# A written-out schedule drawn again: new prices for transfers in the planner, one warm-up matmul fewer, fifteen search seeds in place of four

## The chip, the cores and the metric

One core of one Trainium2 chip runs the whole program in one launch. The metric is the device time of a run in microseconds (us), smaller is better. The kernel before takes 506.23 us as the median of three runs (504.22 to 507.21). TensorE is called PE, VectorE DVE, ScalarE ACT, GpSimd POOL, SyncE SP.

## The reference

Causal attention over 2 batches of 12 heads (448 positions, head size 64), followed by two feed-forward layers over the 896 tokens of 768 features, with 2048 hidden units each:

```python
scores = scale * q @ k.T;  scores = where(mask, -1e9, scores)
attn = exp(scores - max) / (sum + 1e-09);  x = attn @ v          # 896 x 768
h = x @ w_in;  x = (h * clip(h + 3, 0, 6) / 6) @ w_out           # layer 1
h = x @ w_in2; y = (max(h, 0) + alpha * min(h, 0)) @ w_out2      # layer 2
```

## The kernel before

**Precision and tiling.** Scores, transposes and attention products run on PE as f32 matmuls, which the trace shows as two records each. The two layers run on f32r halves: a value is split into a high and a low part, and a product is three matmuls (`three`: high·high, low·high, high·low), each 128 weights columns by 448 tokens. Both layers use a scheme with 7 products of half-size blocks in place of 8, so that blocks of x, of the weights and of the hidden values (`g`) are first added to or subtracted from each other.

**Names.** Attention: `s`, `sl` scores, `e`, `el` their exponentials, `t`, `r` transposes, `a` the transposed exponentials, `o` the output of a head pair. Products into a layer (`w_in`, 8 steps `m`): operands `b11`, `t1`, `t2`, ... against weights `a1`, `s12`, ... in the PSUM banks `a`, `b`, `c`. Products out of a layer (`w_out`) are numbered 1, 2, 7, 6, 4, 5, 3 and run in that order, 72 matmuls each, over operands `x1..`, `x2..`, `x7..` and so on (`x70` to `x77` for product 7; the suffix h or l is the high or the low part) and weights `w1`, `w2`, `w7`, ... into three banks `ya` (products 1, 6, 5, 3), `yb` (2) or `yc` (7, 4). There are 8 banks in all, so the third `yc` bank is the first `yb` bank that comes free: after product 2 DVE adds `yb` to `y` (L770), and frees it.

**Sums.** Before product 7, 6 and 4 the `g` blocks are added to each other in place (`add_g`, 8 sums of 128x448 each), and so are weight blocks. `add_on` (L299 to L312) lets either DVE do such a sum (L309), or POOL issue a transfer that adds on landing (L307). A weight arrives as 64-bit words: SP loads it (`raw`, 768 KB), ACT makes two passes (L262, L265), DVE one (L268), before it is split into halves (ACT L283, DVE L290).

**What sets the order.** Nothing is ordered by hand. Each step is an `Op` with engines it may run on, a price on each of them in us, its operands and a due time. `Plan.solve` walks through a simulated time with these prices: at each step it takes, over all engines, the earliest step that is ready and has its buffers, by due time where several are. `on` with several engines is settled there too. The due times and engine choices of the attention steps (`vary`) are disturbed by random draws, one for each number in `SEEDS`, on top of each other. The resulting list is then emitted, and each engine runs its part of it strictly in order, waiting on semaphores. So a price changes no instruction's work, only where it stands and, for some, on which engine. The prices of transfers are `ISSUE`, `WAIT` and `SHARE` (L64 to L76), read by `lands_at`. Three warm-up matmuls on zeros (`WARM`, L803) stand first on PE.

Of the kernel before, what the change touches and what calls it, by code (L numbers as in the profile page):

```python
# [32 lines left out]
PE, DVE, ACT, POOL, SP = "PE", "DVE", "ACT", "POOL", "SP"  # L33


def f32(t):
    return t.bitcast(F32)
# [12 lines left out]
class Op:  # L50
# [7 lines left out]
    def lands(self, *load, on=SP):  # L58
# [2 lines left out]

ISSUE, WAIT = 0.9, {384: 6.0, 448: 6.5, 768: 7.0}  # L64

TURN = {("r", "r"): 0.05, ("r", "t"): 0.17, ("r", "c"): 0.2, ("r", "q"): 0.15, ("r", "m"): 0.15, ("t", "r"): 0.12,
        ("t", "c"): 0.12, ("t", "q"): 0.1, ("m", "c"): 0.2, ("m", "r"): 0.1, ("m", "q"): 0.1}
LAG = {PE: 0.20, DVE: 0.12, ACT: 0.15, POOL: 0.10, SP: 0.04}
FAR = 1.0e6

SHARE = 3.5

EARLY = 3.0


def lands_at(on, first, us, landed):  # L76

    return max(first, landed[on], min(landed[POOL if on == SP else SP], first + SHARE)) + us

class Plan:
# [30 lines left out]
    def solve(self, slots, strict, overlay, vary=0, seeds=()):  # L113

        for i, o in enumerate(self.ops):
            o.index = i
            for p in o.before:
                p.after.append(o)
        for o in reversed(self.ops):
# [22 lines left out]
        first = {}  # L142
# [4 lines left out]
        queue = {c: sorted((b for b in first if b.cls == c), key=first.get) for c in strict}  # L147
        waiting = {o: len(o.before) for o in self.ops}
        ready = {e: [] for e in LAG}
        clock, landed, port = dict.fromkeys(LAG, 0.7), {SP: 0.0, POOL: 0.0}, 0.0  # L150

        def put(o):
            o.ready = {}
            for e, _ in o.on:
                o.ready[e] = max([p.out + (LAG[p.eng] if p.eng != e else 0.0) for p in o.before], default=0.0)
                ready[e].append(o)

        for o in self.ops:
# [3 lines left out]
        while len(done) < len(self.ops):  # L162
            best = None
            room = {c: queue[c][:len(free[c])] for c in strict}
            for e in LAG:
                can = []
                for o in ready[e]:
                    t = max(clock[e] + TURN.get((mode, o.mode), 0.0) if e == PE else clock[e], o.ready[e])
                    if (e == POOL and e not in o.dma) or (e == DVE and o.port):
                        t = max(t, port)  # L170
                    ok = True
                    need = {}
                    for b in o.bufs:
                        if b.slot is None:
                            need[b.cls] = need.get(b.cls, 0) + 1
                            f = free[b.cls]
                            if len(f) < need[b.cls] or (b.cls in room and b not in room[b.cls]):
                                ok = False
                                break
                            t = max(t, sorted(f)[need[b.cls] - 1][0])  # L180
                    if ok and len(o.on) > 1:
                        def done_by(x, us):
                            late = max(clock[x], o.ready[x], port if (x == POOL and x not in o.dma) or (x == DVE and o.port) else 0.0)
                            late += bias[x] if x != o.on[0][0] else 0.0
                            return lands_at(x, late + o.load[0], o.load[1], landed) if x in o.dma else late + us

                        if POOL in o.dma and done_by(*o.on[0]) + o.on[-1][1] <= o.due - EARLY:
                            ok = e == POOL
                        else:
                            ok = e == min(o.on, key=lambda c: done_by(*c))[0]  # L190
                    if ok:
                        can.append((t, o))
                if can:
                    soon = min(can, key=lambda r: r[0])[0] + hold
                    t, o = min((r for r in can if r[0] <= soon), key=lambda r: (r[1].due, r[1].index))
                    key = (round(t, 2), o.due)
                    if best is None or key < best[0]:
                        best = (key, e, o, t)
            if best is None:
                raise RuntimeError("no step is possible: %s" % [  # L200
                    (e, o.on, [b.name for b in o.bufs]) for e in LAG for o in sorted(ready[e], key=lambda o: o.due)[:4]
                ])
            _, e, o, t = best
            for x, _ in o.on:
                ready[x].remove(o)
            o.eng, o.start = e, t
            mode = o.mode if e == PE else mode
            o.out = o.end = clock[e] = t + dict(o.on)[e]
            if (e == POOL and e not in o.dma) or (e == DVE and o.port):
                port = o.end  # L210
            if o.load and e in o.dma:
                wait, us = o.load
                o.out = landed[e] = lands_at(e, o.start + wait, us, landed)
            for b in [b for b in o.bufs if b.slot is None]:
                f = free[b.cls]
                k = min(range(len(f)), key=lambda i: f[i][0])
                b.slot = f.pop(k)[1]
                if b.cls in strict:
                    queue[b.cls].remove(b)
            for b in o.bufs:  # L220
                b.left -= 1
                b.end = max(b.end, o.out + LAG[e])
                if not b.left:
                    free[b.cls].append((b.end, b.slot))
            if any(b.cls in over_of for b in o.bufs):
                over_left -= 1
                over_end = max(over_end, o.end)
                if not over_left:
                    n = slots[over_cls]
                    free[over_cls] += [(over_end, n + i) for i in range(over_n)]  # L230
            for s in o.after:
                waiting[s] -= 1
                if not waiting[s]:
                    put(s)
            done.append(o)
# [3 lines left out]
class Kernel:  # L239
# [9 lines left out]
    def convert(self, src, sign=1.0, halves=False):  # L249

        nc, op = self.nc, self.plan.op
        raw = Buf("raw", "raw", 2 * DM, U32)
        w = Buf("w", "wf", DM, U32)
        keys = [(w, 0), (w, W3)] if halves else [w]

        def words(k):
            return raw.tile.rearrange("p (n two) -> p n two", two=2)[:, :, k]

        op((SP, 0.45), lambda e: nc.sync.dma_start(out=raw.tile, in_=src), writes=[(raw, "l"), (raw, "h")]).lands(3.2, 2.4)


        op((ACT, 0.80), lambda e: nc.scalar.activation(  # L262
            f32(w.tile), f32(words(1)), AF.Prelu, scale=sign * 2.0 ** -112, alpha=-2.0 ** 32), reads=[(raw, "h")], writes=keys)

        op((ACT, 0.81), lambda e: nc.scalar.activation(  # L265
            words(0), raw.tile.bitcast(U16).rearrange("p (n four) -> p n four", four=4)[:, :, 1],
            AF.Copy, bias=-0.49999, scale=1.0 / 8192.0), writes=[(raw, "l")])
        op((DVE, 0.87), lambda e: nc.vector.scalar_tensor_tensor(  # L268
            out=w.tile, in0=w.tile, scalar=3, in1=words(0), op0=ALU.logical_shift_left, op1=ALU.bitwise_or),
           reads=[(raw, "l")], writes=keys, port=True)  # L270
        return w
# [29 lines left out]
    def add_on(self, out, cols, dst, src, reads, writes, send=0):  # L301

        nc = self.nc

        def emit(e):
            if e == POOL:
                nc.gpsimd.dma_start(out=dst(), in_=src(), accum_op=ALU.add)  # L307
            else:
                nc.vector.tensor_add(dst(), dst(), src())  # L309

        on = [(POOL, ISSUE), (DVE, 0.065 + 0.00105 * cols)]
        self.plan.op(on[:1] if send > 0 else on[1:] if send < 0 else on, emit, reads=reads, writes=writes, port=True).lands(WAIT[cols], 0.0025 * cols, on=POOL)  # L312

    def copy(self, out, src, key, cols, sign=1.0):
        nc = self.nc
# [482 lines left out]
    def build(self):  # L798
        nc, op, d = self.nc, self.plan.op, self.dram
        start, step = 9.0, 5.8  # L800
        warm = Buf("ps", "warm")
        for _ in range(WARM):
            op((PE, 0.9), lambda _: nc.tensor.matmul(  # L803
                warm.tile[:, 0:3 * P], lhsT=self.mask[:, 3 * P:4 * P], rhs=self.mask[:, 3 * P:6 * P], start=True, stop=True),
               writes=[warm], due=-90.0)
        for c in range(KIN):
# [14 lines left out]

SLOTS = {"u": 41, "w": 21, "raw": 3, "kq": 4, "v": 3, "e": 12, "el": 4, "small": 8, "a": 2, "ps": 8, "alpha": 1}
OVER = 38
WARM = 3
SPLIT = (0, 1)
SEND = 0
SCALERS = 2
SEEDS = (21, 21752, 85156, 37451)
ATT = {"kq": 2 * S, "v": 8 * D, "e": 3 * P, "el": 4 * P, "small": 21, "a": 16 * P}


def solve(k):
    return k.plan.solve(SLOTS, ("u", "w", "raw"), ("u", OVER, set(ATT)), k.vary, SEEDS)

# [105 lines left out]
```

## Time and profile before

| | |
|---|---|
| runs: median, lowest, highest | 506.23, 504.22, 507.21 us |
| profiled execution: span from first to last instruction | 502.9 us (the page gives no other time for it) |
| PE busy (matmuls) | 489.1 us, 97% |
| DVE busy | 425.9 us, 85% |
| ACT busy | 390.8 us, 78% |
| POOL busy | 120.8 us, 24% |
| sums as transfers (L307): `g`, weights | 48 and 30 |

The span is the slowest core's time between its first and last instruction; what lies around it in a run is not in the trace. PE is busy nearly throughout, but a matmul's end is modelled, so gaps and the distance from one matmul's start to the next say more than its busy share. The stages follow each other: attention to about 84 us, layer 1 to about 292 us (its `w_out` from 185 us), layer 2 to the end (its `w_out` from 396 us).

### The profile page before, as it was taken

Reading aid. Unit: us, or ns where it says so; the run is one execution under the profiler, and the core shown is the slowest. Engines: PE = TensorE matmul, PEld = TensorE weight load, DVE = VectorE, ACT = ScalarE, POOL = GpSimd, SP = SyncE. Lnnn points to the kernel's source line nnn. Section 1 sums busy time; section 2 is a strip of 40 time slices with the busy share of each in tenths; the row PEclk is TensorE's granted clock in tenths of the full one; section 3 lists DMA queues with packets and bytes.
Section 4 is the critical chain, followed back from the end, with each engine's and each line's share of the span. In section 5 each row is a group of like instructions: output and inputs, shape, how many; then the busy total and the mean of one; then the engine's idle time right before and its main releaser. Section 6 shows DMA issues by size and latency. Waiting matters only on the chain.

```text
span 502.9 us, 7634 instructions
## 1 busy us (share of the span) xinstructions
PE 489.1 (97%) x2598; PEld 427.0 (85%) x2598; DVE 425.9 (85%) x816; ACT 390.8 (78%) x758; POOL 120.8 (24%) x186
## 2 busy tenths in 40 slices
PE   8999999999999999989999999999999999999997
PEld 4666667899999999978998898999999998999996
DVE  5888888999999899698999989777789997999610
ACT  5999999988898999577966668977779995787001
POOL 2757774100012012450001002222200136400000
PEclk9999999999999999999999999999999999999999
DMA  8647302266468559999006229766655799930111
GB/s 283 256 145 231 106 22 69 75 209 205 145 201 243 185 186 261 276 246 227 1 26 176 82 79 244 202 175 176 175 159 191 195 262 271 228 70 1 56 55 55
DMA packets 26486, 81.11 MB, mean 161 GB/s; under 512 B 3024, under 2 KB 14032, under 8 KB 26448
## 3 DMA queue, kind: packets, MB, share of 16 engines
q1 hardware_dynamic: 15216, 61.76, 35.4%
q0 software_dynamic: 11232, 18.88, 21.3%
q8 instruction: 20, 0.33, 0.3%
q14 instruction: 18, 0.15, 0.1%
HBM read 59.00 MB, written 2.75 MB: 123 GB/s over the span
## 4 chain that ended last, share of the span: by engine, by line
PE 32%; DVE 13%; DMA 2%; issue 2%; ACT 2%; DVEq 0%
PE ya L584 11%; PE a L584 9%; PE yc L584 6%; PE c L584 4%; DVE wf L268 2%; DMA g<-g 2%; PE b L584 2%; DVE g L668 1%; DVE w3l L287 1%; DVE w5l L290 1%; DVE w4l L290 1%; DVE g L707 1%; DVE g L650 1%; DVE wf L707 1%; DVE s L618 0%
## 5 line engine op out<-in xcount | busy, mean ns | idle before, releaser
L307 POOL DMA_DIRECT2D g<-g x48 | 42.4, 998 | 150.1 <-DVE g L668 50.6
L268 DVE SCALAR_TENSOR_TENSOR wf<-wf,raw 128x768 uint32<-128x768 uint32 x64 | 60.9, 953 | 8.8 <-ACT wf L262 8.5
L265 ACT ACTIVATE raw<-raw 128x768 uint32<-128x768 uint16 x64 | 58.6, 916 | 3.4 <-DMA raw<-w2i 3.4
L262 ACT ACTIVATE wf<-raw 128x768 f32<-128x768 f32 x64 | 58.0, 911 | 1.8 <-DVE w3l L287 1.8
L307 POOL DMA_DIRECT2D wf<-wf x21 | 18.3, 872 | 123.6 <-DVE s L599 63.9
L452 ACT ACTIVATE e<-e,small 128x128 f32<-128x128 f32 (+2 forms) x72 | 36.1, 511 | 5.8 <-DVE small L447 5.4
L447 DVE CUSTOM_DVE_ANT_0 e<-s,mask 128x256 f32<-128x256 f32 (+2 forms) x72 | 27.1, 418 | 9.4 <-PE s L496 8.6
L476 POOL TENSOR_SCALAR e<-e,small 128x384 f32<-128x384 f32 (+2 forms) x64 | 30.3, 492 | 9.8 <-DVE small L469 8.5
L319 ACT COPY o<-ya 128x448 f32<-128x448 f32 x3 | 1.6, 532 | 32.4 <-PE ya L584 32.4
L565 PEld LDWEIGHTS o<-a,v 128*64 128x64 f32 x192 | 12.8, 136 | 13.1 <-ACT a L547 5.3
L565 PE MATMUL o<-a,v 128*64 128x448 f32 (+3 forms) x192 | 23.4, 386 | 0.2 <-issue 0.2
L496 PE MATMUL s<-kq 64*128 64x384 f32 (+2 forms) x144 | 22.4, 409 | 0.9 <-DMA kq<-kq 0.5
L521 PEld LDWEIGHTS t<-ident,e 128*128 128x128 f32 x144 | 15.8, 141 | 5.6 <-POOL e L476 4.2
L521 PE MATMUL t<-ident,e 128*128 128x128 f32 x144 | 19.3, 278 | 0.9 <-POOL e L476 0.4
L666 ACT ACTIVATE r<-g 128x448 f32<-128x448 f32 x24 | 13.9, 580 | 7.8 <-DVE g L650 7.8
L496 PEld LDWEIGHTS s<-kq 64*128 64x128 f32 x144 | 12.2, 186 | 7.9 <-issue 3.0
L617 ACT CAST s12h<-s 128x768 fp32r<-128x768 f32 x16 | 13.4, 840 | 6.8 <-DVE s L601 6.3
L660 ACT ACTIVATE r<-g 128x448 f32<-128x448 f32 x24 | 13.9, 579 | 5.3 <-DVE g L650 5.1
L618 DVE TENSOR_TENSOR s<-wf,s 128x384 fp32r<-128x384 f32 x32 | 17.6, 553 | 0.0
L618 DVE TENSOR_TENSOR s12l<-s,s12h 128x768 fp32r<-128x768 f32 x16 | 15.6, 974 | 2.4 <-ACT s12h L617 2.4
L668 DVE SCALAR_TENSOR_TENSOR g<-r,alpha,g 128x448 f32<-128x448 f32 x24 | 16.3, 681 | 0.9 <-ACT r L666 0.6
L547 ACT COPY a<-t 128x512 f32<-128x512 f32 x31 | 16.4, 588 | 0.6 <-PE t L521 0.4
(831 smaller groups left out, 1753.2 us busy)
## 6 DMA issues: line engine op xcount, KB each, us to landing
raw<-w1i SPq DMA_DIRECT2D x16, 768.0 KB, 4.7
raw<-w1o SPq DMA_DIRECT2D x16, 768.0 KB, 5.9
raw<-w2i SPq DMA_DIRECT2D x16, 768.0 KB, 5.9
raw<-w2o SPq DMA_DIRECT2D x16, 768.0 KB, 5.9
g<-g POOLq DMA_DIRECT2D x48, 224.0 KB, 9.5
kq<-kq SPq DMA_DIRECT2D x11, 448.0 KB, 5.2
wf<-wf POOLq DMA_DIRECT2D x10, 384.0 KB, 10.7
v<-v SPq DMA_DIRECT2D x12, 256.0 KB, 2.7
```

Source lines behind the costliest of these rows:

```text
L262: op((ACT, 0.80), lambda e: nc.scalar.activation(f32(w.tile), f32(words(1)), AF.Prelu, scale=sign * 2.0 ** -112, alpha=-2.0 ** 32), reads= ...
L265: op((ACT, 0.81), lambda e: nc.scalar.activation(words(0), raw.tile.bitcast(U16).rearrange("p (n four) -> p n four", four=4)[:, :, 1], AF. ...
L268: op((DVE, 0.87), lambda e: nc.vector.scalar_tensor_tensor(out=w.tile, in0=w.tile, scalar=3, in1=words(0), op0=ALU.logical_shift_left, op1 ...
L307: nc.gpsimd.dma_start(out=dst(), in_=src(), accum_op=ALU.add)
L447: nc.vector.tensor_tensor_reduce(out=view(), in0=t.tile[:, off:off + cols], in1=self.mask[:, at:at + cols], scale=-SCALE, scalar=3.0e38, o ...
L452: nc.scalar.activation(view(), view(), AF.Exp, bias=small.tile[:, u:u + 1], scale=-1.0, accum_out=small.tile[:, 7 + u:8 + u])
L476: (nc.gpsimd if e == POOL else nc.vector).tensor_scalar(view(), view(), by, 1.0, ALU.mult, ALU.mult)
L496: nc.tensor.matmul(t.tile[:, off:off + (i + 1) * P], lhsT=kq.tile[rows, S + i * P:S + (i + 1) * P], rhs=kq.tile[rows, 0:(i + 1) * P], star ...
L521: nc.tensor.transpose(t.tile[:, at * P:(at + 1) * P], src.tile[:, off:off + P], self.ident)
L565: nc.tensor.matmul(o.tile[side * D:(side + 1) * D, 0:cols], lhsT=v.tile[:, (2 * kc + side) * D:(2 * kc + side + 1) * D], rhs=a.tile[:, at: ...
L584: nc.tensor.matmul(out, lhsT=t.tile[:, first + at:first + at + P], rhs=rhs.tile, start=start and key is hi and rhs is xh, stop=stop and ke ...
L618: op((DVE, 0.065 + 0.00105 * cols), lambda _: nc.vector.tensor_sub(out(1), src(), f32(out(0))), reads=[*keys, parts[0][0]], writes=[parts[ ...
```

## The change

No step of the computation is altered but one: two warm-up matmuls in place of three. The rest is in the planner: transfers of SP and POOL that overlap now share the queues in fixed parts (`PART`), a transferred sum costs less to issue (0.57), waits 4.0 and moves 1.2 to 2.3 us, and at most 7 of POOL's are in flight (`RING`); such a sum is planned no earlier than 20 us before it is due (`LAZY`), and is given to POOL if it is done 4 us ahead (`EARLY`, was 3); each engine's steps are priced 0 to 5% longer (`PACE`; PE 1% shorter); DVE waits 0.115 us (`DRAIN`) after its own step before a dependent one; PE is at half pace before 4.95 us (`FULL`).

```diff
-ISSUE, WAIT = 0.9, {384: 6.0, 448: 6.5, 768: 7.0}
+ISSUE, WAIT, LOAD, MOVE = 0.57, 4.0, 4.0, {384: 1.2, 448: 1.35, 768: 2.3}
-SHARE = 3.5
-EARLY = 3.0
+PART, TAIL, CALL = {SP: 0.64, POOL: 0.36}, {SP: 0.6, POOL: 1.0}, 0.4
+RING, LAZY, EARLY = 7, 20.0, 4.0
+PACE = {PE: 0.99, DVE: 1.02, ACT: 1.01, POOL: 1.05, SP: 1.0}
+DRAIN, FULL = 0.115, 4.95
 def lands_at(on, first, us, landed):
-    return max(first, landed[on], min(landed[POOL if on == SP else SP], first + SHARE)) + us
+    begin = max(first, landed[on])
+    over = max(0.0, landed[POOL if on == SP else SP] - begin)
+    if us <= over * PART[on]:
+        return begin + us / PART[on], us if over else 0.0
+    return begin + us + over * (1 - PART[on]), over * PART[on]
...
+            o.on = [(e, us * PACE[e]) for e, us in o.on]
...
+                if e == POOL and e in o.dma:
+                    o.ready[e] = max(o.ready[e] + CALL, o.due - LAZY)
...
+                    if e == POOL and e in o.dma:
+                        t = max(t, ring[-RING] + 0.3)
...
+            if e == PE and o.mode and t < FULL:
+                us += min(us, (FULL - t) / 2)
...
-WARM = 3
+WARM = 2
-SEEDS = (21, 21752, 85156, 37451)
+SEEDS = (13117, 66982, 68691, 27780, 6959, 27726, 88620, 72214, 67132, 73300, 90690, 68978, 52530, 59003, 43003)
```

All other instructions are the same in number and shape; 8 transferred sums become DVE sums (2 of `g`, 2 of 128x768 and 4 of 128x384 weights), and some copies, scalings and splits of attention change engine: until the last attention step ACT has 2 instructions more, DVE 1 fewer. Four places show how the rows move.

ACT, layer 1 `w_out`, just ahead of product 7 (`x6..h` are high parts of product 6's operands, each of which waits for a sum by transfer into `g`; `w7h` are product 7's weights). Before:

```order
L283 CAST x60h<-g_1279 128x448
L283 CAST x61h<-g_1422 128x448
L283 CAST x62h<-g_1550 128x448
L283 CAST x63h<-g_1681 128x448
L283 CAST w7h<-wf 128x768
L265 ACTIVATE raw<-raw 128x768
L283 CAST x64h<-g_1813 128x448
L262 ACTIVATE wf<-raw 128x768
L283 CAST w7h<-wf 128x768
```

The same place now:

```order
L299 CAST x60h<-g_1268 128x448
L299 CAST w7h<-wf 128x768
L281 ACTIVATE raw<-raw 128x768
L278 ACTIVATE wf<-raw 128x768
L299 CAST w7h<-wf 128x768
L299 CAST x61h<-g_1419 128x448
L299 CAST x62h<-g_1544 128x448
```

All of product 7's weights now stand ahead of `x61h`, `x62h` and `x63h`; before, three of the four stood behind `x63h` (two of them in these rows).

DVE at the same place, up to the first sum that frees a `yb` bank (`y<-y,yb`). Before:

```order
L290 TENSOR_TENSOR x61l<-g_1422,x61h 128x448
L290 TENSOR_TENSOR w7l<-wf,w7h 128x768
L290 TENSOR_TENSOR x62l<-g_1550,x62h 128x448
L290 TENSOR_TENSOR x63l<-g_1681,x63h 128x448
L290 TENSOR_TENSOR x64l<-g_1813,x64h 128x448
L707 TENSOR_TENSOR wf<-wf 128x768
L268 SCALAR_TENSOR_TENSOR wf<-wf,raw 128x768
L770 TENSOR_TENSOR y_2446<-y_2446,yb_2455 128x448
```

The same place now:

```order
L306 TENSOR_TENSOR x77l<-g_2204,x77h 128x448
L723 TENSOR_TENSOR wf<-wf 128x768
L306 TENSOR_TENSOR x60l<-g_1268,x60h 128x448
L786 TENSOR_TENSOR y_2431<-y_2431,yb_2436 128x448
L306 TENSOR_TENSOR w7l<-wf,w7h 128x768
```

The sum that frees the bank now stands behind `x60l` alone, no longer behind `x61l` to `x64l`. In layer 2 it stands even ahead of `x77l`.

DVE, end of layer 1, up to the sums that free the `ya` banks after product 5 for product 3 (`y<-y,ya`). Before:

```order
L287 SCALAR_TENSOR_TENSOR b2212l<-y_2477,b2212h 128x448
L268 SCALAR_TENSOR_TENSOR wf<-wf,raw 128x768
L290 TENSOR_TENSOR t310l<-t_3108,t310h 128x448
L618 TENSOR_TENSOR s_3149<-wf,s_3149 128x384
L290 TENSOR_TENSOR t311l<-t_3121,t311h 128x448
L290 TENSOR_TENSOR t312l<-t_3126,t312h 128x448
L618 TENSOR_TENSOR s_3176<-wf,s_3176 128x384
L268 SCALAR_TENSOR_TENSOR wf<-wf,raw 128x768
L770 TENSOR_TENSOR y_2763<-y_2763,ya_2290 128x448
```

The same place now:

```order
L303 SCALAR_TENSOR_TENSOR b2210l<-y_2431,b2210h 128x448
L303 SCALAR_TENSOR_TENSOR b2211l<-y_2434,b2211h 128x448
L303 SCALAR_TENSOR_TENSOR b2212l<-y_2450,b2212h 128x448
L786 TENSOR_TENSOR y_2723<-y_2723,ya_2275 128x448
L306 TENSOR_TENSOR t310l<-t_3122,t310h 128x448
```

Of the seven steps that stood between `b2212l` and the sum, none does now.

PE, late in attention (`a<-b11..` and `c<-t10..` are the first products of layer 1). Before:

```order
L521 MATMUL t<-ident,e_930 128x128
L521 MATMUL t<-ident,e_980 128x128
L521 MATMUL t<-ident,e_931 128x128
L521 MATMUL t<-ident,e_981 128x128
L565 MATMUL o<-a,v 64x448 x2
L565 MATMUL o<-a,v 64x320 x2
L565 MATMUL o<-a,v 64x192 x2
L565 MATMUL o<-a,v 64x64 x2
L584 MATMUL a<-b1102h,a1h 128x448
L584 MATMUL a<-b1102l,a1h 128x448
L584 MATMUL a<-b1102h,a1l 128x448
```

PE at the first product of layer 1 now:

```order
L448 MATMUL r<-ident,el 128x128 x8
L600 MATMUL a<-b1100h,a1h 128x448
L600 MATMUL a<-b1100l,a1h 128x448
L600 MATMUL a<-b1100h,a1l 128x448
L600 MATMUL a<-b1101h,a1h 128x448
L600 MATMUL a<-b1101l,a1h 128x448
L600 MATMUL a<-b1101h,a1l 128x448
L600 MATMUL a<-b1102h,a1h 128x448
L600 MATMUL a<-b1102l,a1h 128x448
L600 MATMUL a<-b1102h,a1l 128x448
L436 MATMUL sl<-kq 64x448 x4
```

The first products stand together in one group, with about a quarter of attention's matmuls still behind them. Over PE's whole attention part, the kind of matmul (scores, `sl`, transposes, `o`, layer products) changes 61 times in the order before and 44 times now; 12 matmuls of layer 1 stand ahead of the last attention matmul before, 24 now.

## Rows read from the trace of the kernel before

**Rows 1.** The page's span and busy time: busy us (share) xinstructions by engine.
```profile
span 502.9 us, 7634 instructions
PE 489.1 (97%) x2598; PEld 427.0 (85%) x2598; DVE 425.9 (85%) x816; ACT 390.8 (78%) x758; POOL 120.8 (24%) x186
```

**Rows 2.** Stretches from:to in us, then busy us by engine, PEclk, DMA share.
```profile
10.00:80.00 70.00, 67.74 (x523) 43.58 (x522) 59.05 (x233) 68.47 (x219) 48.98 (x91) 1.00 0.46 152
84.40:200.00 115.60, 115.47 (x573) 106.56 (x568) 111.52 (x181) 105.12 (x177) 16.20 (x20) 1.00 0.62 189
200.00:300.00 100.00, 95.46 (x468) 87.32 (x467) 91.31 (x142) 71.54 (x119) 16.48 (x19) 1.00 0.54 136
430.00:499.00 69.00, 69.00 (x342) 64.03 (x341) 44.01 (x66) 28.86 (x50) 3.47 (x4) 1.00 0.29 70
```

**Rows 3.** PE's 9 matmuls of one product, from the chain: start, us.
```profile
348.42 1.82 PE a L584 x9
```

**Rows 4.** PE's waits: us in total, times, longest.
```profile
PE yc L584 <- DVE y L770: 3.5, 2, 2.3
PE ya L584 <- DVE y L770: 1.8, 1, 1.8
PE ya L584 <- DVE w6l L290: 0.5, 1, 0.5
PE a L584 <- DVE g L650: 0.3, 1, 0.3
```

**Rows 5.** PE at layer 1's product 7: start, length, instruction, [idle before].
```profile
214.86 0.37 PE L584 MATMUL yc<-x70l,w7h 128*128 128x448 f32 x1
215.06 0.37 PE L584 MATMUL yc<-x70h,w7l 128*128 128x448 f32 x1
217.76 0.47 PE L584 MATMUL yc<-x70h,w7h 128*128 128x448 f32 x1 [2.33 <-DVE y L770]
```

**Rows 6.** DVE ahead of the first sum that frees a yb bank.
```profile
212.65 0.96 DVE L290 TENSOR_TENSOR w7l<-wf,w7h 128x768 fp32r<-128x768 f32 x1 [4.48 <-ACT w7h L283]
213.53 0.62 DVE L290 TENSOR_TENSOR x62l<-g,x62h 128x448 fp32r<-128x448 f32 x1
...
217.09 0.61 DVE L770 TENSOR_TENSOR y<-y,yb 128x448 f32<-128x448 f32 x1
```

**Rows 7.** ACT in the same stretch.
```profile
208.32 0.57 ACT L283 CAST x62h<-g 128x448 fp32r<-128x448 f32 x1 [2.59 <-DMA g<-g]
211.32 0.57 ACT L283 CAST x63h<-g 128x448 fp32r<-128x448 f32 x1 [2.44 <-DMA g<-g]
211.79 0.83 ACT L283 CAST w7h<-wf 128x768 fp32r<-128x768 f32 x1
```

**Rows 8.** Transfers issued 95 to 140 us: count, KB each, median us to landing.
```profile
g<-g POOLq DMA_DIRECT2D x4, 224.0 KB, 3.3
```

**Rows 9.** Transfers issued 195 to 232 us.
```profile
g<-g POOLq DMA_DIRECT2D x16, 224.0 KB, 11.7
raw<-w1o SPq DMA_DIRECT2D x3, 768.0 KB, 9.2
raw<-w2i SPq DMA_DIRECT2D x3, 768.0 KB, 8.3
```

**Rows 10.** DVE ahead of the sums that free the ya banks, end of layer 1.
```profile
272.18 0.62 DVE L287 SCALAR_TENSOR_TENSOR b2212l<-y,b2212h 128x448 fp32r<-128x448 f32 x1
272.71 0.95 DVE L268 SCALAR_TENSOR_TENSOR wf<-wf,raw 128x768 uint32<-128x768 uint32 x1
...
276.99 1.68 DVE L770 TENSOR_TENSOR y<-y,ya 128x448 f32<-128x448 f32 x3
```

**Rows 11.** Weight sums that DVE does before (L309): busy us, mean ns.
```profile
L309 DVE TENSOR_TENSOR wf<-wf 128x768 f32<-128x768 f32 (+1 forms) x19 | 16.1, 849 | 0.3
```

**Rows 12.** PE in mid-attention.
```profile
44.12 1.53 PE L521 MATMUL t<-ident,e 128*128 128x128 f32 x12
45.57 0.49 PE L496 MATMUL s<-kq 64*128 64x128 f32 x4
...
50.60 0.60 PE L432 MATMUL r<-ident,el 128*128 128x128 f32 x4
51.04 0.60 PE L521 MATMUL t<-ident,e 128*128 128x128 f32 x4
```

**Rows 13.** PE at the start.
```profile
1.30 3.99 PE L803 MATMUL warm<-mask 128*128 128x384 f32 x6 [1.30 <-DVE mask L861]
5.22 2.22 PE L496 MATMUL s<-kq 64*128 64x384 f32 x16
```

**Rows 14.** The first transfer, issued at 0.72 us: us to landing.
```profile
kq<-kq SPq DMA_DIRECT2D x1, 448.0 KB, 3.4
```

**Rows 15.** PE at the last group of attention.
```profile
82.59 1.95 PE L565 MATMUL o<-a,v 128*64 128x448 f32 x16
```

**Rows 16.** The last operands of layer 1's first products on DVE.
```profile
71.46 1.26 DVE L618 TENSOR_TENSOR s12l<-s,s12h 128x768 fp32r<-128x768 f32 x1
74.79 0.62 DVE L290 TENSOR_TENSOR b1102l<-o,b1102h 128x448 fp32r<-128x448 f32 x1
```

More of the change, by code (lines that the diff above doesn't have):

```diff
@@ L60, in lands @@
         self.load, self.dma = load, (on,)
-ISSUE, WAIT = 0.9, {384: 6.0, 448: 6.5, 768: 7.0}
-TURN = {("r", "r"): 0.05, ("r", "t"): 0.17, ("r", "c"): 0.2, ("r", "q"): 0.15, ("r", "m"): 0.15, ("t", "r"): 0.12,
+ISSUE, WAIT, LOAD, MOVE = 0.57, 4.0, 4.0, {384: 1.2, 448: 1.35, 768: 2.3}
+TURN = {("r", "r"): 0.065, ("r", "t"): 0.17, ("r", "c"): 0.2, ("r", "q"): 0.19, ("r", "m"): 0.15, ("t", "r"): 0.12,
         ("t", "c"): 0.12, ("t", "q"): 0.1, ("m", "c"): 0.2, ("m", "r"): 0.1, ("m", "q"): 0.1}
@@ L149, in solve @@
         ready = {e: [] for e in LAG}
-        clock, landed, port = dict.fromkeys(LAG, 0.7), {SP: 0.0, POOL: 0.0}, 0.0
+        clock, landed, port, ring = dict(dict.fromkeys(LAG, 0.7), PE=1.3), {SP: 0.0, POOL: 0.0}, 0.0, [0.0] * RING
         def put(o):
@@ L154, in put @@
             for e, _ in o.on:
-                o.ready[e] = max([p.out + (LAG[p.eng] if p.eng != e else 0.0) for p in o.before], default=0.0)
+                o.ready[e] = max([p.out + (LAG[p.eng] if p.eng != e else DRAIN if e == DVE else 0.0) for p in o.before], default=0.0)
+                if e == POOL and e in o.dma:
+                    o.ready[e] = max(o.ready[e] + CALL, o.due - LAZY)
                 ready[e].append(o)
@@ L184, in done_by @@
                             late += bias[x] if x != o.on[0][0] else 0.0
-                            return lands_at(x, late + o.load[0], o.load[1], landed) if x in o.dma else late + us
+                            return lands_at(x, late + o.load[0], o.load[1], landed)[0] + TAIL[x] if x in o.dma else late + us
                         if POOL in o.dma and done_by(*o.on[0]) + o.on[-1][1] <= o.due - EARLY:
@@ L207, in solve @@
             mode = o.mode if e == PE else mode
-            o.out = o.end = clock[e] = t + dict(o.on)[e]
+            us = dict(o.on)[e]
+            if e == PE and o.mode and t < FULL:
+                us += min(us, (FULL - t) / 2)
+            o.out = o.end = clock[e] = t + us
             if (e == POOL and e not in o.dma) or (e == DVE and o.port):
@@ L212, in solve @@
                 wait, us = o.load
-                o.out = landed[e] = lands_at(e, o.start + wait, us, landed)
+                landed[e], back = lands_at(e, o.start + wait, us, landed)
+                landed[POOL if e == SP else SP] += back
+                o.out = landed[e] + TAIL[e]
+                if e == POOL:
+                    ring.append(o.out)
             for b in [b for b in o.bufs if b.slot is None]:
@@ L257, in words @@
             return raw.tile.rearrange("p (n two) -> p n two", two=2)[:, :, k]
-        op((SP, 0.45), lambda e: nc.sync.dma_start(out=raw.tile, in_=src), writes=[(raw, "l"), (raw, "h")]).lands(3.2, 2.4)
+        op((SP, 0.45), lambda e: nc.sync.dma_start(out=raw.tile, in_=src), writes=[(raw, "l"), (raw, "h")]).lands(LOAD, 2.5)
         op((ACT, 0.80), lambda e: nc.scalar.activation(
@@ L311, in add_on @@
         on = [(POOL, ISSUE), (DVE, 0.065 + 0.00105 * cols)]
-        self.plan.op(on[:1] if send > 0 else on[1:] if send < 0 else on, emit, reads=reads, writes=writes, port=True).lands(WAIT[cols], 0.0025 * cols, on=POOL)
+        self.plan.op(on[:1] if send > 0 else on[1:] if send < 0 else on, emit, reads=reads, writes=writes, port=True).lands(WAIT, MOVE[cols], on=POOL)
     def copy(self, out, src, key, cols, sign=1.0):
@@ L802, in build @@
         for _ in range(WARM):
-            op((PE, 0.9), lambda _: nc.tensor.matmul(
+            op((PE, 1.4), lambda _: nc.tensor.matmul(
                 warm.tile[:, 0:3 * P], lhsT=self.mask[:, 3 * P:4 * P], rhs=self.mask[:, 3 * P:6 * P], start=True, stop=True),
```

## Prediction

> **What bounds the kernel now.** I read the page's busy shares first: PE 97%, DVE 85%, ACT 78% of a span of 502.9 us [rows 1]. That says PE, but the ends of matmuls are modelled, so the next view was the table by stage [rows 2]. It shows four stages with four limits. From 10 to 80 us (attention) PE and ACT are both at 97 to 98% of the stretch. From 84 to 200 us PE has hardly a gap, with DVE at 96%. From 200 to 300 us, where layer 1 leaves and layer 2 begins, PE lacks 4.5 us of 100, and DVE is at 91% although it has work queued. From 430 us PE is busy for 69.00 of 69.00 us. PE's matmul of a layer starts every 0.20 us where nothing waits (9 in 1.82 us) [rows 3]. As every matmul of the layers stays, what the change can give is in three places only: PE's waits in the layers, the pace of attention, and the start.
>
> The table of PE's waits [rows 4] names them: nearly all are on DVE sums. The two longest of `yc` (2.3 and 1.2 us) are the third `yc` bank, which must be freed by the first sum of `yb`; one of 1.8 us is the `ya` bank before product 3. A wait costs more than its idle time: in [rows 5] matmuls start 0.20 us apart, and then one starts 2.70 us after the last, 2.50 lost for 2.33 idle. I add 0.17 to each of the others: 1.4, 2.0, 0.7 and 0.5, together 7.1 us.
>
> The cause of the longest is in the timelines, read backwards. DVE's sum of `yb` starts at 217.09; ahead of it DVE stood 4.48 us for one `w7h` of ACT [rows 6]. ACT did that `w7h` at 211.79, after it had stood for `x62h` and `x63h`, 2.59 and 2.44 us, each for a sum by transfer [rows 7]. Such a sum lands 3.3 us after its issue in a quiet stretch [rows 8], but 11.7 us in this one, where 16 of them and six weight loads are on the way [rows 9]. The order before was drawn with 6.5 us for it. So a transfer that was late held ACT, ACT held DVE, and DVE held PE, none of it needed by the sum that PE waited for.
>
> By the Trainium skill's page "DMA: Bandwidth & Descriptors" (section on the anatomy of one DMA), a transfer issued by GpSimd takes some 2.0 us plus its bytes at 436 GB/s, which is 2.5 us for 224 KB by my estimate; the quiet row comes near it, the burst is almost five times that, and the measurement decides; the rule gets no chance of its own. If the page's figure held in the burst, the old price would have been ample, no row would be late for it, and the two terms of `yc` below would be nothing: 503.7 in place of 499.8.
>
> **The change part by part.**
>
> *yc banks.* In the order now, all of `w7h` stand ahead of `x61h` on ACT, and the `yb` sum stands behind `x60l` alone on DVE (in layer 2 ahead of `x77l`). What it still needs from transfers is `x60`, whose sum is issued first of the eight, about 15 us of DVE steps ahead; even at 11.7 us it is there. So both waits go: -2.5 and -1.4. Bounds: nothing gained, if the burst has become longer, to -3.9.
>
> *ya bank before product 3.* The sum stands now directly behind `b2212l`; before, seven steps lay between, from 272.71 to 276.99, 4.3 us [rows 10], and PE waited 1.8. But DVE has the same work to do in the stretch as a whole (84 rows in place of 82 between the first `yb` sum and this one), and what is left out here was done sooner or comes later. I take -1.5, between 0 and -2.0. The waits for `w6l` and `g` (0.7 and 0.5) I leave as they are.
>
> *Sums moved to DVE.* Eight more, at 0.85 us each if all are like the mean of the whole ones [rows 11]; three of them in layer 1's `w_out`, where DVE is at 91%: 2.5 us if nothing hides them. The five in layer 2 have DVE's slack there to lie in. Behind a longer DVE queue stand the splits for the next product and the sums that free banks. Against it, three transfers fewer in the worst burst. I take +1.0 for new waits of any kind, between -0.5 (the burst shrinks) and +2.5. Where the first `g` sums of a layer now queue on POOL behind a weight sum of the seventh step, I take nothing: they were issued through the layer before, and are now issued together some 30 us before `x70` reads them; eight at the burst's spacing fit.
>
> *Attention.* A change of the kind of matmul costs PE time: four transposes between transposes take 0.44 us (50.60 to 51.04), so 12 would take 1.32, and before a score they take 1.45 (44.12 to 45.57) [rows 12], 0.13 more. There are 17 such changes fewer: -2.2. The cover is thin: ACT is at 98% [rows 2], and does two steps more before attention's last, which are partly work for the layer that it would do later anyway. I take +0.7 back; the bounds are +2.7 (ACT sets the end of attention, and neither turns nor the start count) and -2.3 (PE's idle time of attention, 70.00 less 67.74, goes as well).
>
> *The start.* Six records of three warm-up matmuls run from 1.30 to 5.22, 0.65 us each [rows 13]; four end at 3.9. The first operand lands at 0.72 + 3.4 = 4.1 us [rows 14], so the first score can start about 1.0 us sooner. The table of stretches prints a granted clock of 1.00 throughout [rows 2], so I take the level at the start from the pace: the warm-up's 384 columns at 0.65 us are the lower level of the clock (1.2 GHz); the 16 score records after it, of 128 to 384 columns, take 2.22 us in all, which is the upper (2.4). If the rise stays where it was, near 5 us, the time gained runs at half pace: -0.5. Bounds: -1.0, and +1.5 if PE's idle 0.2 to 0.3 us before the first score puts the rise off by as long again as it took (some 3.5 us at half pace, less what is gained).
>
> The Trainium skill's page "TensorE: Matmul & The Clock Gate" (Part 1) speaks for that last bound: the slow rate is the default, and activity of the array releases it. No row here shows a warm-up with a gap behind it; by the page the start could lose 1.5 us in place of gaining 0.5, and the sum be 501.8; I count that with the first rival below, which ends at the same time.
>
> **The sum.** -0.5 - 2.2 + 0.7 - 2.5 - 1.4 - 1.5 + 1.0 = -6.4: the profiled span goes from 502.9 to 496.5. The median of the runs shown, 506.23, is 3.3 above that span (the lowest run 1.3, the highest 4.3); I keep the 3.3: 499.8 us.
>
> **The rivals.** *ACT holds attention:* it is the other engine at 98%, and was not relieved; then start and turns give nothing, -4.4, 501.8 us. Against it: 12 more layer matmuls stand inside attention, so a PE that waits for ACT has them to do.
>
> *The waits move:* DVE is at 96% from 84 to 200 and 91% after, so that it, not the late transfers, sets when layer 1 ends; a wait removed at product 7 comes back at 6 or 3. Then the layers give nothing and only attention's -2.0 is left: 504.2 us. For it: the same DVE work between the sums. Against it: DVE stood 4.48 us in one place for nothing it needed.
>
> *All goes well:* start -1.0, turns -2.2, attention's idle -2.3, all five waits -7.1, nothing new: about -12.6 at most; two thirds of the surplus over the forecast gives 495.7 us.
>
> *Slower:* the first product's nine matmuls now stand on PE with a quarter of attention behind them, some 20 us before its last group starts at 82.6 [rows 15], so by my estimate at about 64 us. Before, its last operand `b1102l` was done at 75.4 [rows 16]. PE takes its rows in order, so if ACT or DVE brings that operand no sooner, PE, and with it all of attention behind, stands for up to 11 us: 499.8 + 11 = 511 us. It decides from a wait of 9 us on. For it: attention was the part with the least slack. Against it: the operand's place on ACT and DVE has moved forward as well.
>
> **How the numbers follow.** Forecast (497.8 to 501) 0.49; ACT holds attention 0.18; the waits move 0.15; all goes well 0.10; slower 0.08. A measurement can tell some 0.5% from no change, 2.5 us: under 503.7 is faster, over 508.8 slower. So faster is 0.49 + 0.18 + 0.10 = 0.77, same 0.15, slower 0.08. The range, 495.6 to 504.6, takes in all cases but the slower one and the edges of the others.
>
> **What would show it.** Right: no wait of `yc` on `y` over 0.3 us in either layer, DVE without a stop before `w7l`, the `ya` wait under 0.6; the first score at 4.2 us; the last `o` of attention within 2 us of 82.6 with 24 layer matmuls before it. Wrong: a wait of PE in front of the first `a<-b11`, waits of `ya` for `w6l`, `w4l` or `w5l` that were not there, transfers of `g` that land over 15 us after issue, a first score later than 5.2 us, or a clock that rises after 6 us.

## The result, and the profile after

The changed kernel takes **496.9 us** (median; 496.4 to 497.4), the one before 506.0 beside it: 0.983 of it, interval 0.980 to 0.986. Forecast were 499.8, within 495.6 to 504.6. A second set of runs, on another occasion, gave 500.7 against 506.2 (0.986, 0.981 to 0.991); the last section has what is known of that. The profiled spans, 502.9 and 495.4, differ by **7.5 us**, and it is these 7.5 that the steps below add up to; the medians differ by 9.1, mainly because the profiled run of the kernel before was one of its quicker ones.

Page of the changed kernel, busy us by engine (answers to [rows 1]):

```profile
span 495.4 us, 7593 instructions
PE 484.7 (98%) x2596; PEld 426.9 (86%) x2596; DVE 430.8 (87%) x823; ACT 388.4 (78%) x755; POOL 115.5 (23%) x182
```

The same kernel by stretches (to [rows 2]): us, busy us by engine, PEclk, DMA share.

```profile
10.00:80.00 70.00, 66.35 (x523) 45.40 (x521) 58.24 (x228) 66.93 (x214) 48.14 (x96) 1.00 0.46 153
84.00:200.00 116.00, 114.71 (x570) 104.73 (x571) 111.64 (x181) 103.19 (x174) 14.73 (x16) 1.00 0.60 185
200.00:300.00 100.00, 100.00 (x494) 92.38 (x493) 95.69 (x150) 75.68 (x126) 16.00 (x19) 1.00 0.51 130
```

Two things are to be seen. From 200 to 300 us PE, which lacked 4.5 us, lacks nothing: 494 matmuls in place of 468. And in attention PE is busy for *less* of the stretch than before, 66.35 in place of 67.74, though ACT is too.

The longest of PE's waits behind the warm-up (to [rows 4]): us in total, times, longest.

```profile
PE r L448 <- POOL el L492: 1.8, 3, 1.1
PE o L581 <- ACT a L563: 1.3, 1, 1.3
PE r L448 <- DVE small L463: 1.1, 1, 1.1
PE s L512 <- DMA kq<-kq: 0.7, 1, 0.7
PE a L600 <- DVE a L634: 0.3, 1, 0.3
```

No `yc`, no `ya`, no `w6l` is left; what remains, but for the 0.3 of `a`, lies in attention, where `r` and `o` now wait.

DVE of the changed kernel at product 7 (to [rows 6]):

```profile
210.01 0.62 DVE L306 TENSOR_TENSOR x77l<-g,x77h 128x448 fp32r<-128x448 f32 x1
210.55 0.95 DVE L723 TENSOR_TENSOR wf<-wf 128x768 f32<-128x768 f32 x1
211.41 0.62 DVE L306 TENSOR_TENSOR x60l<-g,x60h 128x448 fp32r<-128x448 f32 x1
212.11 0.62 DVE L786 TENSOR_TENSOR y<-y,yb 128x448 f32<-128x448 f32 x1
212.65 0.95 DVE L306 TENSOR_TENSOR w7l<-wf,w7h 128x768 fp32r<-128x768 f32 x1
```

The sum `y<-y,yb` comes 5 us sooner (217.09 before), and no stop of 4.48 us stands ahead of it. The burst it has to live with has shrunk as well (to [rows 9]; 195 to 232 us, count, KB each, median us to landing):

```profile
g<-g POOLq DMA_DIRECT2D x14, 224.0 KB, 7.9
raw<-w1o SPq DMA_DIRECT2D x4, 768.0 KB, 6.5
raw<-w2i SPq DMA_DIRECT2D x3, 768.0 KB, 8.3
```

Two measures serve below. *Late in the layers*: from the matmul behind attention's last `o` to the last matmul, less 0.2028 us for each of the layer matmuls in it. *Length of attention*: from the first score to that first matmul, less 0.2028 us for each layer matmul done inside, less half of the stretch in which the first scores ran at the clock's lower level (the trace's record of the granted clock rises at 4.95 us before and at 6.04 in the changed kernel). The stretch views print PEclk 1.00 there; the scores show it themselves, 8 in one microsecond of the changed kernel and 14 in the next (us, PE busy on `s`, PEclk, DMA share):

```profile
5.00:6.00 1.00, 1.00 (x8) 1.00 1.03 310
6.00:7.00 1.00, 1.00 (x14) 1.00 1.09 331
```

| us | before | changed |
|---|---|---|
| first score + half of the slow stretch | 5.22 + 0 | 4.17 + 0.94 |
| length of attention | 76.81 | 76.91 |
| late in the layers | 8.40 | 0.96 |

The differences, -0.1, +0.1 and -7.4, make the 7.4 to 7.5. PE, from the last steps of attention, of before and then of the changed kernel (to [rows 15]):

```profile
84.47 0.47 PE L584 MATMUL c<-t101h,s12h 128*128 128x448 f32 x1
```
```profile
83.31 0.37 PE L600 MATMUL a<-t201h,s12l 128*128 128x448 f32 x1
85.00 1.95 PE L581 MATMUL o<-a,v 128*64 128x448 f32 x16 [1.31 <-ACT a L563]
86.88 0.47 PE L600 MATMUL a<-t202h,s12h 128*128 128x448 f32 x1
```

84.47 with 12 layer matmuls done and 86.88 with 24: 2.41 later and 12 x 0.2028 = 2.43 ahead, the same.

### The profile page after: what moved, and what is told of

It reads as the page before. It is cut to its first block, busy times and chain, and to the rows that moved or that the text cites. A ratio compares the mean times of both kernels' runs of the same rounds, so it can differ in the third digit from the quotient of the medians.

```text
span 495.4 us, 7593 instructions
## 1 busy us (share of the span) xinstructions
PE 484.7 (98%) x2596; PEld 426.9 (86%) x2596; DVE 430.8 (87%) x823; ACT 388.4 (78%) x755; POOL 115.5 (23%) x182
## 4 chain that ended last, share of the span: by engine, by line
PE 91%; ACT 4%; DVE 4%; issue 1%; POOL 0%; DVEq 0%; ACTq 0%
PE ya L600 24%; PE a L600 23%; PE yc L600 12%; PE c L600 11%; PE yb L600 6%; PE b L600 6%; PE t L537 3%; PE o L581 3%; PE s L512 3%; ACT e L468 2%; ACT a L563 1%; PE warm L819 1%; DVE e L463 1%; DVE e L492 1%; PE r L448 1%
## 5 line engine op out<-in xcount | busy, mean ns | idle before, releaser
L323 POOL DMA_DIRECT2D g<-g x46 | 41.3, 1308 | 95.4 <-DVE x70l L306 18.6
L323 POOL DMA_DIRECT2D wf<-wf x17 | 16.1, 979 | 161.7 <-ACT r L676 52.2
L468 ACT ACTIVATE e<-e,small 128x384 f32<-128x384 f32 (+2 forms) x72 | 36.0, 510 | 6.2 <-DVE small L463 5.9
L463 DVE CUSTOM_DVE_ANT_0 e<-s,mask 128x384 f32<-128x384 f32 (+2 forms) x72 | 26.4, 417 | 7.6 <-PE s L512 5.5
L492 POOL TENSOR_SCALAR e<-e,small 128x256 f32<-128x256 f32 (+2 forms) x65 | 30.1, 480 | 10.9 <-DVE small L485 5.6
L512 PE MATMUL s<-kq 64*128 64x256 f32 (+2 forms) x144 | 21.1, 413 | 1.0 <-DMA kq<-kq 0.7
L512 PEld LDWEIGHTS s<-kq 64*128 64x128 f32 x144 | 13.3, 195 | 9.5 <-DVE small L463 4.2
L325 DVE TENSOR_TENSOR wf<-wf 128x768 f32<-128x768 f32 (+1 forms) x23 | 19.1, 829 | 0.2
L633 ACT CAST a1h<-wf 128x768 fp32r<-128x768 f32 x16 | 13.4, 837 | 3.7 <-DVE wf L284 3.6
```

What stands on the lines that cost most here:

```text
L463: nc.vector.tensor_tensor_reduce(out=view(), in0=t.tile[:, off:off + cols], in1=self.mask[:, at:at + cols], scale=-SCALE, scalar=3.0e38, o ...
L468: nc.scalar.activation(view(), view(), AF.Exp, bias=small.tile[:, u:u + 1], scale=-1.0, accum_out=small.tile[:, 7 + u:8 + u])
L492: (nc.gpsimd if e == POOL else nc.vector).tensor_scalar(view(), view(), by, 1.0, ALU.mult, ALU.mult)
L512: nc.tensor.matmul(t.tile[:, off:off + (i + 1) * P], lhsT=kq.tile[rows, S + i * P:S + (i + 1) * P], rhs=kq.tile[rows, 0:(i + 1) * P], star ...
```

## The experiments

The diffs are cut to the lines that matter; what stands behind a # is a remark.

**One knot untied by hand.** Theory: a late transfer held ACT, ACT held DVE, DVE held PE.

```diff
 # before, both layers: the splits of x62, x63, x64 (ACT h, DVE l) behind the first yb sum
+        order = [o for o in order if o not in moved]
+        at = order.index(first) + 1
+        order[at:at] = moved
```

> The kernel before, with one thing changed by hand: in both layers the six split operations of x62, x63 and x64 (three copies on ACT, three subtractions on DVE) are put behind the first yb sum instead of ahead of it; all else keeps its order and no work is removed. Theory (a slow transfer holds ACT's copy, that holds DVE in its order, and DVE holds the sum that TensorE waits for): both waits for yc go, 2.5 and 1.4 us, and nothing else moves, so the time falls by 3.9 from 506.0 to about 502. Rival (VectorE simply has too much work in this stretch, whatever its order): the waits move to a later product and the time stays within 1 us of before, 505 to 507.

505.7 us, ratio 0.999 (0.996 to 1.001), a time that the rival had named. Both waits of `yc` are gone, and another has grown; waits of PE in this kernel:

```profile
PE ya L584 <- DVE w6l L290: 2.1, 1, 2.1
PE ya L584 <- DVE y L770: 1.7, 1, 1.7
```

So of 3.5 us of `yc`, 1.6 came back at `w6l` (0.5 before). The profiled layers are 8.6 late, but 2.9 of that lies between 270 and 440 us, where each matmul took 0.207 in place of 0.203 (see the last section); without it 5.7, 2.7 less than before. Mechanism as the theory has it, size between it and the rival. The interval of the time holds -2.2 to +0.7 and can't tell this gain from none.

**The transfers themselves.**

```diff
 # before, both layers: the g sums that feed x62, x63, x64 on DVE
+            last.eng = DVE
```

> The kernel before, with the three sums of products that feed x62, x63 and x64 added by VectorE instead of by a transfer, in both layers; order of all else kept. Theory (the transfer's lateness is the cause): the yc waits of 2.5 and 1.4 us go, although VectorE gets three more sums of 0.85 us a layer, because the stall of 4.48 us ahead of the yb sum goes with them: 502 to 503. Rival (VectorE's work bounds the stretch): three more sums make the waits longer, by up to 2.5 us in each layer, 507 to 511.

501.7 us, ratio 0.989 (0.986 to 0.993). With three DVE sums *more* a layer PE waits less:

```profile
PE ya L584 <- DVE y L770: 2.0, 1, 2.0
PE ya L584 <- DVE w6l L290: 0.7, 1, 0.7
```

No `yc` is left, `w6l` gave 0.2 back, and the layers are 4.8 late, 3.6 less than before; the time is just below the 502 to 503 of the theory. That the stretch is bound by DVE's work is refuted; by what DVE stood for, it was.

**Which part of the planner.** Three kernels, each with part of the change: the new transfers alone (`lands_at`, `RING`, `LAZY`, `WAIT`, `MOVE`, and the price of a load) in the kernel before; everything new but the seeds; everything new but the transfers. The margin `EARLY` goes with the transfers in all three: 4.0 in the first, although its expectation speaks of old margins, and 3.0 in the last.

```diff
 # new transfers alone: before with
+ISSUE, WAIT, LOAD, MOVE = 0.57, 4.0, 4.0, {384: 1.2, 448: 1.35, 768: 2.3}
+RING, LAZY, EARLY = 7, 20.0, 4.0
 # old seeds: changed kernel with
+SEEDS = (21, 21752, 85156, 37451)
 # old transfers: changed kernel with
+ISSUE, WAIT, LOAD, SHARE = 0.9, {384: 6.0, 448: 6.5, 768: 7.0}, 3.2, 3.5
+RING, LAZY, EARLY = 1, FAR, 3.0
```

> The kernel before with only the new accounting of transfers in its planner (two rings that share the engines, in-flight limit, later landing), its own seeds, the old margins and three warm-up matmuls. Theory (the planner put sums on transfers that land later than it believed, and that is nearly the whole loss in the layers): the layers' waits of about 7.3 us go down to 1 to 3, and the time comes to 500 to 502. Rival (the gain comes from the wider margins, the in-place sums or the new seeds): the time stays within 1.5 us of before, 504.5 to 507.

> The changed kernel with the four old seeds of the search; transfers' accounting, margins and two warm-up matmuls as changed. Theory (the accounting of transfers gives the layers' gain, and the new search gives next to nothing, as its fewer turns in attention were used up by new waits): the layers lose 1 to 3 us over 0.2028 us a matmul, as with the transfers alone (1.5) and as changed (2.6), and the time is within 1 us of the changed kernel, 496 to 498. Rival (the search anew carries a good part): the layers lose 4 or more, or the last attention step ends 2 us later at the same count of layer matmuls, and the time is 499 to 501.

> The changed kernel with the old accounting of transfers (a sum lands 6 to 7 us after issue, no limit in flight), all else as changed, the new seeds too. Theory (the accounting is nearly the whole gain): sums by transfer land late again, the layers lose 5 to 9 us in place of 2.6, and the time is 500 to 504. Rival (margins and seeds would do it alone): the layers lose under 4 us, and the time is under 499.

| | median | ratio to before | span | late in the layers | length of attention |
|---|---|---|---|---|---|
| transfers alone | 498.3 | 0.984 (0.978 to 0.989) | 496.2 | 1.3 | 76.9 |
| old seeds | 497.8 (a further run: 505.9) | 0.984 (0.978 to 0.989) | 495.7 | 1.0 | 77.7 |
| old transfers | 507.2 | 1.002 (0.999 to 1.005) | 503.2 | 9.3 | 76.1 |

The new accounting of transfers alone gives 7.1 of the layers' 7.4 us, at a time better than the 500 to 502 expected, and without it nothing is gained at all, by neither the seeds nor the longer prices of the engines' steps. Which part of the accounting does it (the shared queues, the limit in flight, `LAZY`, `EARLY`) was not taken apart. With the old seeds the layers and the span are those of the changed kernel, but attention is 0.7 longer; a start 0.5 us sooner, where the clock rose at 4.8 us, hides it. The new accounting does not make the transfers quick: where it stands alone the burst still takes 11.2 us for each of 16,

```profile
g<-g POOLq DMA_DIRECT2D x16, 224.0 KB, 11.2
```

and the largest wait of a `ya` bank is 0.2 us:

```profile
PE ya L595 <- DVE y L781: 0.2, 1, 0.2
```

Nor does it issue them sooner: POOL issues the first eight of the burst between 195.8 and 207.9 us in this kernel, between 195.9 and 205.1 before. What it moves is their readers. ACT of this kernel, which waits for no `g` here (before: 205.2, 208.3 and 211.3, the last two after 2.59 and 2.44 us of idle [rows 7]):

```profile
208.14 0.57 ACT L294 CAST x61h<-g 128x448 fp32r<-128x448 f32 x1
211.82 0.56 ACT L294 CAST x62h<-g 128x448 fp32r<-128x448 f32 x1
216.16 0.56 ACT L294 CAST x63h<-g 128x448 fp32r<-128x448 f32 x1
```

In `Plan.solve`'s own simulated time the eight sums that feed `x60` to `x67` land 7.6 to 9.9 us after issue in the kernel before, and 9.0 to 12.7 in this one; the planner, told that they are late, puts other work ahead of what reads them.

At 507.2 the last is above the 500 to 504 expected. One of its waits cost more than its length; PE at the end of layer 1, and then stretches (us, busy by engine, PEclk, DMA share):

```profile
274.25 0.36 PE L596 MATMUL ya<-x57h,w5l 128*128 128x448 f32 x1
278.05 0.47 PE L596 MATMUL ya<-x30h,w3h 128*128 128x448 f32 x1 [3.44 <-DVE y L782]
...
280.03 0.58 PE L596 MATMUL ya<-x30h,w3l 128*128 128x448 f32 x1
280.40 0.58 PE L596 MATMUL ya<-x31h,w3h 128*128 128x448 f32 x1
```
```profile
274.00:278.00 4.00, 0.61 (x4) 0.23 (x2) 3.96 (x8) 0.75 (x2) 0.00 (x0) 1.00 0.64 209
279.50:282.80 3.30, 3.30 (x11) 2.94 (x10) 3.30 (x8) 2.79 (x6) 0.00 (x0) 0.50 0.56 147
```

After 3.44 us of idle the granted clock stood at the lower level from 279.5 to 282.8, and matmuls started 0.37 us apart: eight at 0.17 more and one on each side, 1.6 us on top. The wait of 2.33 us in the kernel before has no such row behind it: PEclk is 1.00 from 200 to 300 us [rows 2, 5]. That is one run: of the 46 other runs of that kernel on record 27 have a mean granted clock of 0.992 to 0.998 (the profiled run here, with its one such stretch, has 0.997), while the nine of the changed kernel have 0.999 or 1.0; no trace shows where it fell in those. The Trainium skill's page "TensorE: Matmul & The Clock Gate" (section on oscillation) tells of waits that drop the clock; the row from 279.5 us agrees.

**The start.**

```diff
             o.emit(o.eng)
+            if o is next(q for q in order if q.eng == PE):
+                o.emit(o.eng)
```

> The changed kernel with a third matmul on zeros again, all else in its order. Theory (two warm-up matmuls let the first score start 1.05 us earlier, but the granted clock then rises 1.1 us later, so the head gains nothing): with the third the scores start near 5.2, the clock rises near 5.0, and the time stays within 0.5 us of the changed kernel, 496.5 to 497.4. Rival (the warm-up is plainly on the path, each worth its time): 0.5 to 1 us slower, 497.5 to 498.

500.2 us, ratio 0.986 (0.981 to 0.992), span 496.6. PE at the start, of the changed kernel and then with the third:

```profile
4.17 3.77 PE L512 MATMUL s<-kq 64*128 64x384 f32 x24
```
```profile
5.44 3.71 PE L512 MATMUL s<-kq 64*128 64x384 f32 x24
```

The 24 scores take as long, so the clock rose not sooner but later, at 7.2 in place of 6.0 us: the theory, by which it would rise near 5.0, has fallen. Attention and layers are the same to 0.1 us (76.84, 0.97), and the whole 1.2 us of the span is in the start. The time is outside both ranges; two of its four runs are near 498 us and two above 502, so it can't decide, and the span is one pair (see the start, below).

**Where the turns' gain went.** In both kernels the scaling of the softmax is left out, all other rows kept.

```diff
-        op((DVE, 0.2), lambda _: nc.vector.reciprocal(r(small), r(small)), writes=[(small, 14 + lo)])
+        op((DVE, 0.2), lambda _: None, writes=[(small, 14 + lo)])
...
             def scale(e, view=view, u=u):
+                return
```

> The kernel before without the scaling of attention's weights by one over their sum (the small sum with 1e-9, the reciprocal and the scalings are left out), every other instruction in its order. It is the yardstick for the same done to the changed kernel: DVE, ACT and POOL have less to do between a score and its transposes, so most of TensorE's idle time of attention (some 2.5 us) should go, and what is left is issue and turns. Both theories expect attention to end 2 to 4 us sooner than with the scaling, about 81 to 83 us with 12 matmuls of the layers done.

> The changed kernel with the same scaling left out, every other instruction in its order. Theory (17 fewer changes of the kind of matmul do save some 2 us, but TensorE waits for the softmax chain in their place): with the chain shortened the waits go, from about 5.8 us to under 3.5, and attention, counted at the same number of layer matmuls done, ends 1.5 to 2.5 us ahead of the kernel before treated alike. Rival (changes of kind cost nothing that an order could save): no difference beyond 0.7 us between the two, as it was with the scaling.

First matmul after attention, of before and then of the changed kernel, each so treated:

```profile
5.46 2.88 PE L496 MATMUL s<-kq 64*128 64x384 f32 x14
...
84.50 0.47 PE L584 MATMUL c<-t101h,s12h 128*128 128x448 f32 x1
```
```profile
4.18 3.89 PE L512 MATMUL s<-kq 64*128 64x384 f32 x24
...
81.79 1.95 PE L581 MATMUL o<-a,v 128*64 128x448 f32 x16 [0.69 <-ACT a L563]
83.67 0.47 PE L600 MATMUL a<-t202h,s12h 128*128 128x448 f32 x1
```

Before: 84.50 - 5.46 - 12 x 0.2028 - 1.01 (half of the slow stretch) = 75.6. Changed: 83.67 - 4.18 - 24 x 0.2028 - 1.06 = 73.6. Two us between them, where with the scaling there was 0.1 the other way; the idle time of PE in attention is 2.4 us in both (with the scaling 2.8 before, 5.6 changed). So the changed order does save 2 us of PE's work in attention, and waits for the scaling and what hangs on it had taken them back. The two orders differ in more than the 17 changes of kind, so that these are the cause is an inference, but two things agree with it. 17 at 0.13 us [rows 12] are 2.2. And with the scaling left in, the length of attention less PE's idle time is 74.0 before, 73.9 with the old seeds and 74.1 with the transfers alone, orders with 59, 57 and 59 changes behind the warm-up, against 71.3 in the changed kernel and 72.0 with the old transfers, which have 42 and 41. The first kernel did not get the 2 to 4 us shorter that was expected, only 1.2; the second 3.3. Whole times (505.8 us; 494.3 and 502.4 in the two runs of the second) say no more than the spans here.

**Can it be had?** One `r` and the last `o` are relieved by hand.

```diff
+    pe[101:106] = pe[103:106] + pe[101:103]        # nine b110. matmuls ahead of r
+    act.insert(act.index(third) + 1, split)        # b2202h behind the copies for o
```

> The changed kernel with two moves by hand in attention: on PE the first nine matmuls of layer 1 (the three b110. groups) stand ahead of the eight r matmuls that wait 0.47 us, and on ACT the step b2202h, which waits for DVE, stands behind the three copies that the last o waits for. Theory (PE's waits in attention come from single steps of the softmax chain that stand behind others, not from an engine that is full): the wait before the last o falls from 1.3 to 0.2 to 0.5 us, that before r goes, attention counted at the same number of layer matmuls ends 1.0 to 1.6 us sooner, and the span is 493.8 to 494.6 beside the changed kernel's 495.4. Rival (ACT is full, so what PE gets sooner in one place it waits for in another): under 0.4 us in all.

> The changed kernel once more, unaltered, on the chip and beside the runs that the kernel above is timed with. Expected: 496 to 498 us, a granted clock that rises somewhere between 4.4 and 7.5 us from the start though the first score starts at 4.2 again, and layers that lose 0.9 to 1.1 us behind attention, as in its first profile.

504.2 us (0.994 of before, 0.990 to 0.997), against 500.7 for the unaltered kernel in the same set: slower. The unaltered kernel missed its 496 to 498 as well; its layers are 4.3 late, and 3.3 of that is a slower pace (see the last section), which the altered one has in the same stretch. Waits of PE with the two moves:

```profile
PE a L621 <- DVE g L687: 1.8, 1, 1.8
PE a L621 <- DVE small L484: 1.3, 1, 1.3
PE o L602 <- ACT a L584: 0.2, 1, 0.2
```

The wait of `o` went from 1.3 to 0.2 as expected, and two new ones came: `a<-b1100h` waits 1.3 us for a DVE step that reads scores (its bank, by the releaser), and behind attention a matmul waits 1.8 us for a `g` sum of DVE; which of DVE's steps makes that late was not taken apart. Attention is 77.9 long against 76.9, and the layers are 6.4 late against 4.3. The rival's outcome holds and more, though not for its reason: what PE gained in one place it lost in others, by the releasers to a bank and to DVE, not to ACT. No kernel with the whole computation has a shorter profiled span than the changed kernel.

## Why the prediction came out as it did

The mechanism was right: a faster kernel, by the layers, because late transfers had held DVE's order. By terms:

- *yc banks* (-2.5, -1.4): right. Both waits are gone, DVE has no stop, and the two hand edits to these places alone bring 2.7 and 3.6 in the layers. One reading was off: the old planner priced a `g` sum not at 6.5 us but at 6.5 and 1.1 for the move, and up to 9.9 in this burst; it was late all the same.
- *ya bank* (-1.5): right in kind, a little small; the wait is gone whole, 1.8 and 0.17 of restart.
- *w6l and g* (left at 0.7 and 0.5) and *new waits from the eight sums moved* (+1.0): wrong. The old waits went, and no new one of note came (the 0.3 of `a` that the list has stands at 94 us, where the kernel before started a matmul 0.3 late too), although DVE is now at 95.7% from 200 to 300 us. This is the term that was mis-sized, and with the two waits left in the sum it is the larger part, some 2 us, of the 3.0 by which the layers' 4.4 fell short of 7.4; the `ya` bank has 0.5 more, and the rest is in smaller steps that were not taken apart. I had put a price on DVE's added work in a stretch where it had stood idle for transfers.
- *Attention* (-2.2 + 0.7 = -1.5): wrong, +0.1. The -2.2 is borne out (2.0 in the kernels without scaling), the +0.7 was not 0.7 but 2.1 to 2.8 in waits. I looked at ACT's busy share, which fell; the waits are for single steps, `el` on POOL, a score's maximum on DVE, a copy on ACT. Of the rival "ACT holds attention" the outcome for attention was right and the reason was not.
- *The start* (-0.5): -0.1 between the two profiles. Over six profiled runs with three warm-up matmuls and six with two, first score plus half the slow stretch averages 5.74 and 5.22, so the means differ by 0.5 as forecast, but the values scatter by more (4.99 to 6.48 and 4.56 to 5.62): neither the -0.5 nor the -0.1 of one pair is clear of that. The bound of +1.5 from a gap behind the warm-up shows in no run as such.
- *Around the span*: I added 3.3; the median of the changed kernel is 1.5 above its profiled span. The 3.3 was no constant: each run of both kernels lies 1.7 to 1.9 above its own span, and the rest of the 3.3 was a profiled run quicker than the median (502.9, where the 46 other runs of that kernel have spans of 502.0 to 508.7).
- *Slower*: the first `a<-b11` group ran at 61.8 without a wait; refuted.

The sum: 1.1 us less of span than the 496.5 forecast, and 1.8 less around it, make 496.9 of 499.8. That the span came so near is in part luck: the layers gave 3.0 more than forecast, attention and the start 2.0 less. Two of the prediction's own signs spoke against it: the last `o` began at 85.0, more than 2 us from 82.6, and the clock rose after 6 us, at 6.04.

## What to carry to other kernels

When a planner puts work on transfers, its price for a late transfer decides more than its search: with the new price the old seeds came within 0.3 us of span (0.7 longer in attention), with the old price the new seeds gained nothing. Look at what an engine stands for before pricing work added to it. And a saving on PE in a latency chain is not a saving until the chain behind it is shown to be shorter: take the chain's steps out once and see whether the saving appears.

## What the runs showed of the hardware

**The clock's rise does not follow the warm-up here.** In twelve profiled runs it rose between 4.5 and 7.5 us, with three warm-up matmuls at 4.5, 5.0, 5.7, 6.3, 7.2 and 7.5, with two at 4.8, 6.0, 6.3, 6.4, 6.7 and 7.0; the same instructions gave 6.0 and 7.0. The Trainium skill's page "TensorE: Matmul & The Clock Gate" (Part 1) has the rise not tied to a count of matmuls, and different from run to run of one kernel, which this agrees with. Half of the difference is lost: up to 1.5 us between two of these runs.

**A matmul's pace falls by 2% at full granted clock.** The changed kernel, first profile and then the second, in one stretch of pure layer work:

```profile
120.00:140.00 20.00, 20.00 (x101) 18.52 (x100) 19.54 (x33) 18.73 (x32) 0.00 (x0) 1.00 0.49 161
```
```profile
120.00:140.00 20.00, 20.00 (x98) 18.18 (x97) 19.22 (x33) 18.51 (x31) 0.00 (x0) 1.00 0.47 159
```

101 matmuls and 98 (those that overlap an edge counted), both with PE busy throughout and PEclk 1.00; from start to start they are 0.203 and 0.207 us apart. In the second run this lasts from about 80 to 280 us and costs 3.3 of the 4.0 us by which the spans differ (495.4, 499.4). It is PE alone: from 100 to 280 us DVE's low halves of 128x448 take 617 and 619 ns on average and ACT's high halves 565 and 564. It shows in four of the twelve profiles: from 80 to 280 us in the two of the last set, from 230 to 500 and from 270 to 440 us in two others. It may be why medians here wander by 4 us between occasions, with the changed kernel's granted clock at 0.999 or 1.0 in both sets; runs without a trace can't show it. So the steps were read from spans and waits rather than from medians; what brings it about is open.
